# A new order table that moves forty plain transfers from SyncE's queue to ScalarE's, in a fused attention and gated-MLP kernel

## The chip, the core and the metric

The kernel runs on one core of a Trainium2 chip. The metric is the device time of one launch in microseconds (us). Five engines of the core take part: TensorE (PE, matrix products), VectorE (DVE), ScalarE (ACT), GpSimd (POOL) and SyncE (SP). SyncE computes nothing here: it only issues DMA transfers, one after the other, in program order. ScalarE issues transfers too, in its own program order and among its own arithmetic. Each engine takes its instructions strictly in the order in which the program lists them, so an instruction that waits holds back everything behind it on its engine.

## What is computed

```python
# q, k, v: (8, 12, 448, 64); w_in (768, 1024); conv_w (3, 1024); w_out (1024, 768)
q_n = q / sqrt(mean(q*q, -1) + 1e-6) * g_q          # the same for k with g_k
scores = q_n @ k_n.T / sqrt(64)
attn = exp(scores - max);  attn = attn / (sum(attn) + 1e-9)
x = (attn @ v).transpose(0, 2, 1, 3).reshape(8, 448, 768)
h = maximum(x @ w_in, 0)
conv_out = conv_w[0]*h[s-1] + conv_w[1]*h[s] + conv_w[2]*h[s+1]    # over the tokens s
out = (h * sigmoid(conv_out)) @ w_out               # (8, 448, 768), float32
```

## The kernel before

**Tiling.** The 96 heads are taken two at a time: 48 head pairs n = 0..47, six to a batch b. Pairs 0 to 9 work in float32 with their transposes on TensorE. From pair 10 on, everything that TensorE multiplies is split into two float16 parts (a rounded part and the remainder), and the transposes are done by DMA. A pair's probabilities are made in seven slots j of 128 rows. When a batch's six pairs are done, its tokens go through the MLP: a product with w_in (`in_part`, L1054), relu and the three-tap convolution (`in_relu`, L1062/L1064, and L1074), a gate through tanh (L1080), the product with w_out (`out_part`, L1123), the evacuation of the result (`out_evac`, L279/L281) and the store (`out_store`, L1137). Attention of later pairs and the MLP of earlier batches are interleaved, so that TensorE has matrix products from both.

**The path of one slot of probabilities** (pairs 10 on):

- `scores` (L836) multiplies q and k into a PSUM bank; `soft_max` (L842, DVE) takes the row maximum; `soft_exp` (L850, ACT) writes the exponentials into a tile `e` (ring of 4).
- `p_hi` (L855, recorded under the helper line L275, nearly always ACT) rounds `e` to float16 into the first half of a buffer `ph`; `p_lo` (L860, recorded under L287 as two instructions, POOL or DVE) puts the remainder into the second half.
- `p_turn` (L870, always SP) issues the DMA that transposes the `ph` buffer into the tile `PT`; after the last slot `pv` (L970) multiplies `PT` with v.
- `ph` has **four** buffers, used in turn by all slots. So `p_hi` of a slot can't start before the `p_turn` four slots earlier has landed.

`q_turn` (L700) is the same kind of transposing DMA for q, one for each pair from 10 on, also always on SP. There are 266 `p_turn` and 38 `q_turn`.

**Plain transfers.** All other transfers may be issued by SP or by ACT, as the table says for each of them (`issuer`): the loads of k and v (`load_k`, `v_load`, both L548), of q (`load_q`, L557 or L559), the softmax sums' way through memory to spread them over the partitions (`sum_store` L912, `sum_load` L926 from pair 10 on and L930 before), and the results (`out_store`). Before, 119 of them are issued by ACT.

**Completion semaphores.** Every transfer, of whichever engine, gets one of eight completion semaphores (DMAHW0 to DMAHW7), in turn, in program order. Before a transfer is issued, its engine has to know that the transfer eight places earlier, which used the same semaphore, has landed. Where an earlier wait of that engine doesn't already say so, the issue itself waits for it.

**What sets the order.** Nothing is scheduled while the kernel is built. The table `ORDER` (L20 on) has four characters for each of the 5038 steps: two name the step, one the engine, one the PSUM banks. It is decoded at L1248 to L1261, and L1268 to L1280 emit the steps in just that order. Each engine executes its steps as they come in the table. The code that matters for the steps spoken of later:

```python
phbuf = [const.tile([P, 2 * S], F16, name=f"ph{i}") for i in range(BUFS["ph"])]   # ph=4
...
def issuer(*step):
    return nc.scalar if on[step] == "ACT" else nc.sync
...
a, b, e, z = (DIGITS.index(x) for x in ORDER[4 * i : 4 * i + 4])
fn, args = plan[len(DIGITS) * a + b]
step, e = (fn.__name__, *args), ("PE", "DVE", "ACT", "POOL", "SP")[e]
order.append((step, fn))
on[step] = e
```

## Time and profile before

| | us |
|---|---|
| median of 3 runs | 843.84 |
| the three runs | 842.46, 843.84, 849.87 |
| the profiled execution, its own time | 841.89 |
| its span, first to last instruction | 840.0 |
| PE busy in the span | 770.5 (92%) |
| DVE busy | 706.2 (84%) |
| ACT busy | 677.3 (81%) |
| POOL busy | 467.2 (56%) |

How to read it: the three runs are timed without a profile; the profiled execution is a fourth one, and every row of the trace is of it. "Busy" counts arithmetic only. Issuing transfers isn't counted as busy, so SP has no busy time here; how long it is occupied is seen from the rows of its queue (SPq), where the duration of a transfer is the time that the *issue* takes on the engine, not the time to landing. In the same way ACTq is a transfer that ACT issues. In timelines and lists of waits, "[2.42 <-X]" says that the engine stood idle for 2.42 us before the instruction and that X ended the wait. The page divides the 840 us into 40 slices; in it, PE has something to do nearly everywhere, and no engine is full everywhere.

### The profile page before, as it was taken

What the parts mean: (1) busy time and instruction counts of PE and PEld (TensorE: products, weight loads), DVE (VectorE), ACT (ScalarE), POOL (GpSimd) and SP (SyncE); (2) the same over time, 40 slices, a digit from 0 to 9 for tenths busy, and PEclk for the clock granted to TensorE, in tenths of its full rate; (3) what the DMA queues carried; (4) which work ended last, traced back from release to release, by engine and by line L of the source; (5) the groups of instructions that cost most, each with busy time, mean ns of one, the idle gap of its engine ahead of it and who ended that gap; (6) DMA issues with size and microseconds to landing.
All of it is one profiled execution on the core that took longest, in us unless ns stands there. A gap on an engine that the chain in (4) does not pass through costs nothing.

```text
span 840.0 us, 16991 instructions
## 1 busy us (share of the span) xinstructions
PE 770.5 (92%) x5278; PEld 410.1 (49%) x5278; DVE 706.2 (84%) x1589; ACT 677.3 (81%) x1590; POOL 467.2 (56%) x758
## 2 busy tenths in 40 slices
...
GB/s 226 231 169 121 192 157 86 83 160 194 185 160 173 175 193 176 166 156 175 198 168 165 172 207 175 173 158 171 170 173 143 164 169 171 121 120 143 19 1 76
DMA packets 355246, 130.88 MB, mean 156 GB/s; under 512 B 297532, under 2 KB 351572, under 8 KB 355156
## 3 DMA queue, kind: packets, MB, share of 16 engines
...
## 4 chain that ended last, share of the span: by engine, by line
DMA 23%; ACT 21%; PE 18%; DVE 17%; POOL 9%; issue 8%; SPq 2%; ACTq 2%; POOLq 0%; DVEq 0%
DMA PT<-ph 17%; ACT e L850 7%; PE bank L1123 6%; POOL ph L287 5%; PE bank L1054 5%; ACT ph L275 4%; PE bank L970 3%; PE bank L836 3%; PE bank L878 2%; DMA qkf<-in_k_dram 2%; ACT sq L578 2%; DVE st L590 1%; DVE ph L287 1%; ACT bank L1062 1%; DVE vacc L744 1%
## 5 line engine op out<-in xcount | busy, mean ns | idle before, releaser
L287 POOL TENSOR_TENSOR ph<-e,ph 128x384 f16<-128x384 f32 x360 | 214.7, 623 | 90.1 <-ACT ph L275 37.0
L1054 PE MATMUL bank<-x,wi 128*128 128x448 f16 x1152 | 231.3, 356 | 3.1 <-ACT e L850 3.1
L1123 PE MATMUL bank<-wo,gring 128*128 128x384 f16 (+1 forms) x1056 | 197.2, 328 | 5.0 <-ACT e L850 2.1
L275 ACT CAST ph<-e 128x448 f16<-128x448 f32 x250 | 137.7, 565 | 47.2 <-DMA PT<-ph 42.7
L1054 PEld LDWEIGHTS <-wi 128*128 128x128 f16 x1152 | 111.4, 99 | 113.0 <-issue 19.0
L836 PE MATMUL bank<-kT,qT 64*128 64x448 f16 (+3 forms) x1072 | 140.3, 396 | 19.9 <-ACT e L850 11.2
L1123 PEld LDWEIGHTS <-gring 128*128 128x128 f16 (+1 forms) x1056 | 101.5, 99 | 75.2 <-issue 21.6
L287 POOL TENSOR_TENSOR sq<-qkf,st 112x512 f32<-112x512 f32 (+1 forms) x68 | 70.7, 1047 | 49.9 <-issue 14.4
L970 PE MATMUL bank<-PT,vp 128*64 128x448 f16 x836 | 87.0, 354 | 7.0 <-ACT e L850 4.7
L287 DVE TENSOR_TENSOR ph<-e,ph 128x384 f16<-128x384 f32 (+1 forms) x172 | 60.9, 396 | 19.7 <-ACT ph L275 17.6
L590 DVE TENSOR_REDUCE st<-sq 128x16 f32<-128x1024 f32 (+2 forms) x50 | 58.2, 1168 | 17.9 <-ACT sq L578 17.6
L970 PEld LDWEIGHTS <-vp 128*64 128x64 f16 x836 | 53.8, 109 | 38.8 <-issue 19.7
L836 PEld LDWEIGHTS <-qT 64*128 64x128 f16 (+1 forms) x912 | 35.0, 97 | 77.0 <-issue 57.1
L578 ACT ACTIVATE sq<-qkf 128x1024 f32<-128x1024 f32 (+2 forms) x47 | 48.1, 1024 | 18.6 <-DMA qkf<-in_k_dram 10.8
L658 PE MATMUL bank<-ident,sq 128*128 128x128 f32 (+1 forms) x232 | 35.3, 278 | 23.5 <-DVE sq L287 15.7
L287 POOL TENSOR_TENSOR qkf<-sq,qkf 112x512 f16<-112x512 f32 x34 | 39.4, 1160 | 16.0 <-ACT qkf L275 11.3
L1123 PE MATMUL bank<-wo,wi 128*128 128x384 f16 (+1 forms) x192 | 46.9, 326 | 0.0
L878 PE MATMUL bank<-ident,e 128*112 128x128 f32 x280 | 40.7, 284 | 6.0 <-ACT e L850 3.9
L658 PEld LDWEIGHTS bank<-ident,sq 128*128 128x128 f32 (+1 forms) x232 | 26.5, 143 | 35.8 <-issue 17.4
L878 PEld LDWEIGHTS bank<-ident,e 128*112 128x112 f32 x280 | 31.2, 137 | 23.1 <-ACT e L850 9.4
L287 POOL TENSOR_TENSOR x<-x,x 128x448 f16<-128x448 f32 x31 | 32.2, 1038 | 15.2 <-DVE rsum L900 3.2
L275 ACT COPY PT<-bank 112x512 f32<-112x512 f32 x66 | 36.9, 592 | 2.6 <-PE bank L878 2.6
...
## 6 DMA issues: line engine op xcount, KB each, us to landing
...
PT<-ph SPq DMA_TRANSPOSE x266
...
```

The lines of the kernel that those rows point to most:

```text
L275: (nc.scalar.copy if e == "ACT" else elementwise(e).tensor_copy)(dst, src)
L287: elementwise(e).tensor_tensor(dst, a, b, op=op)
L578: nc.scalar.activation(sq, x, AF.Square)
L590: nc.vector.tensor_reduce(st, sq, axis=AX.X, op=ALU.add)
L658: nc.tensor.transpose(ps[:, t * w : (t + 1) * w], x[:, t], ident[:w, :w])
L744: nc.vector.tensor_reduce(keyed(n, old("vacc", b))[:, i : i + 1], keyed(n, old("v", n)).rearrange("p h t d -> p (h t d)"), axis=AX.X, op=A ...
L836: nc.tensor.matmul(ps[u][o, :S], lhs, rhs, start=(i == 0), stop=(whole(m) or i == 2),)
L850: nc.scalar.activation(fixed("e", (n, j), ebuf)[:, :S], held["s", (n, j)][:, :S], AF.Exp, bias=old("sst", (n, j)), accum_out=old("rsum", n ...
L878: nc.tensor.transpose(ps[:w, kt * P : (kt + 1) * P], e[:, kt * w : (kt + 1) * w], ident)
L970: nc.tensor.matmul(ps[HALF[h], :S], lhs, pt[:, k, h * S : (h + 1) * S], start=(i == 0 and j == 0), stop=(i == pvs(n)[-1] and j == NB - 1),)
L1054: nc.tensor.matmul(ps[:, :S], wi[:, wl, c, fc * P : (fc + 1) * P], old("x", b * NP + c)[:, xl], start=(i == 0), stop=(i == 3 * NP - 1),)
L1123: nc.tensor.matmul(ps[p0 : p0 + m, :NO2], g, wo[:, wl, fc, half * NO2 : (half + 1) * NO2], start=(i == 0), stop=(i == 3 * NFC - 1),)
```

## The change

Only the table `ORDER` is new; no function and no buffer changes. Both tables hold the same 5038 steps. Three things differ:

- **Issuers.** 90 plain transfers (as steps of the table) move from SP to ACT and 50 from ACT to SP: 159 instead of 119 are issued by ACT. Between the first and the last `p_turn`, SP has 198 plain DMA instructions in its order before and 149 after (`p_turn` and `q_turn` not counted), ACT 104 and 153.
- **Places.** Steps stand in another order. Most of the moved transfers stand later behind the release of the buffer that they fill, or behind the step whose result they store.
- **Engines of arithmetic.** 245 of the other steps change engine, in both directions and nearly in balance: 73 from DVE to POOL and 70 back, 39 from ACT to DVE and 32 back, 19 from POOL to ACT and 12 back.

```diff
--- before.py
+++ after.py
 ORDER = (
-    "$6&!$8$!!!#!$9#!$7&!$C$!$:#!$;#!$<%!$=%!$D#!$E#!$>#!!:&!!>#!$?#!$T&!$F#!$G%!$U#!%$&!%&$!%%&!$@%!"
...
+    "$6&!$8$!!!#!$7&!$C$!!:&!$9#!$:#!$;#!$<%!$=%!$D#!$E#!!>#!$F#!$>#!!?#!$G#!$?#!$H%!$T&!$U#!%$&!%&$!"
...
 )
```

What that does to the engines' queues is shown at three places.

**First place: SP, at head pair 21.** SP's instructions from the end of pair 20's `p_turn`s into those of pair 21. `PT_20`/`PT_21` is the transposed tile of the pair, `ph0` to `ph3` the four buffers of the ring, `qkf` the float32 tiles of q and k, `v4`/`v5` tiles of v, `rd` the memory through which the softmax sums go, `row` the tile that they come back to. Before:

```order
L870 DMA_TRANSPOSE PT_20_3990<-ph0_77 128x7x128
L548 DMA qkf1_86<-in_k_dram 64x2x256
L870 DMA_TRANSPOSE PT_21_4182<-ph1_78 128x7x128
L557 DMA qkf1_86<-in_q_dram 112x2x128 x2
L548 DMA v4_92<-in_v_dram 64x2x256
L548 DMA v4_92<-in_v_dram 64x2x192
L1137 DMA out_0_dram<-c_('o'_1_3_1_4066 128x384
L700 DMA_TRANSPOSE qT_23_4220<-qkf2_87 128x8x112
L870 DMA_TRANSPOSE PT_21_4182<-ph2_79 128x7x128
L870 DMA_TRANSPOSE PT_21_4182<-ph3_80 128x7x128
L548 DMA qkf2_87<-in_k_dram 64x2x256
L912 DMA rd_20_4309<-rT_20_4283 4x32x32
```

and after:

```order
L870 DMA_TRANSPOSE PT_20_3980<-ph0_77 128x7x128
L548 DMA qkf1_86<-in_k_dram 64x2x192
L557 DMA qkf1_86<-in_q_dram 112x2x128 x2
L870 DMA_TRANSPOSE PT_21_4212<-ph1_78 128x7x128
L870 DMA_TRANSPOSE PT_21_4212<-ph2_79 128x7x128
L700 DMA_TRANSPOSE qT_23_4252<-qkf2_87 128x8x112
L870 DMA_TRANSPOSE PT_21_4212<-ph3_80 128x7x128
L870 DMA_TRANSPOSE PT_21_4212<-ph0_77 128x7x128
L870 DMA_TRANSPOSE PT_21_4212<-ph1_78 128x7x128
L548 DMA qkf2_87<-in_k_dram 64x2x256
L548 DMA v5_93<-in_v_dram 64x2x256
L912 DMA rd_21_4366<-rT_21_4314 4x32x32
```

Before, two loads of q, two of v, a store and a `q_turn` stand between the first and the second `p_turn` of pair 21. After, nothing stands between these two, and only the `q_turn` between the second and the third. The loads of v and the store that stood here have moved, some of them to ACT.

**Second place: ACT, at head pairs 34 to 36.** ACT's instructions with what each waits for; DMAHW is one of the eight completion semaphores. Before:

```order
L850 ACTIVATE e0_81,rsum0_96<-bank6_72,sst_(36_0_7368 128x448 [waits DVE_49]
L548 DMA qkf1_86<-in_k_dram 64x2x256 [waits DMAHW6_49]
L275 CAST ph1_78<-e3_84 128x448 [waits DMAHW0_49,Activation_49]
L850 ACTIVATE e1_82,rsum0_96<-bank3_69,sst_(36_1_7394 128x448 [waits DVE_49,Pool_49]
L926 DMA row0_98<-rd_34_7268 4x1x448 [waits DMAHW2_49]
L275 CAST ph2_79<-e0_81 128x448 [waits DMAHW1_49,Activation_49]
L275 CAST ph3_80<-e1_82 128x448 [waits Activation_49]
```

and after:

```order
L850 ACTIVATE e3_84,rsum1_97<-bank6_72,sst_(35_6_7315 128x448 [waits DVE_49,Activation_49,Pool_49]
L926 DMA row0_98<-rd_34_7264 4x1x448 [waits DMAHW6_49,DMAHW5_49]
L275 COPY vp_34_7135<-vp_34_7135 64x2x64
L275 COPY carry_102<-gring_101 128x2x64 x2
L850 ACTIVATE e0_81,rsum0_96<-bank2_68,sst_(36_0_7322 128x448 [waits DVE_49,Activation_49,Pool_49]
L548 DMA qkf1_86<-in_k_dram 64x2x256
L275 CAST ph0_77<-e2_83 128x448 [waits DMAHW7_49,Activation_49]
L275 CAST ph1_78<-e3_84 128x448 [waits DMAHW0_49,Activation_49]
L1137 DMA out_0_dram<-c_('o'_4_1_0_7221 128x384
```

The `sum_load` of pair 34 (L926) has moved up by two exponentials and now waits for two semaphores. The load of k, which waited for a semaphore before, waits for nothing after.

**Third place: DVE, up to the first product that TensorE needs.** L397, L401 and L405 convert one part of a weight, L590 to L632 make the root mean squares of q and k (tile `st`), L1173 and L1174 the gains, and L287 with the tile `sq` scales q and k; TensorE's first transposes need that. The rows go up to the first scaling. Before (one L397 stands further ahead):

```order
L401 SCALAR_TENSOR_TENSOR wi32_99<-wo32_100,wi32_99 128x512
L617 SCALAR_TENSOR_TENSOR st_0_111<-st_0_111 112x8 x2
L405 SCALAR_TENSOR_TENSOR wi32_99<-wo32_100,wi32_99 128x512
L590 TENSOR_REDUCE st_1_141<-sq_1_142 112x8
L1173 TENSOR_TENSOR G_75<-gqk_74 128x1
L1174 TENSOR_SCALAR G_75<-G_75 128x1
L617 SCALAR_TENSOR_TENSOR st_0_111<-st_0_111 112x8 x2
L625 TENSOR_SCALAR st_1_141<-st_1_141 112x8
L287 TENSOR_TENSOR sq_0_112<-qkf0_85,st_0_111 112x2x4x64
```

and after (a first L397, L401 and L405 stand further ahead):

```order
L397 TENSOR_SCALAR wi32_99<-wo32_100 128x512
L617 SCALAR_TENSOR_TENSOR st_0_111<-st_0_111 112x8
L623 TENSOR_SCALAR st_1_143<-st_1_143 112x8
L617 SCALAR_TENSOR_TENSOR st_0_111<-st_0_111 112x8
L401 SCALAR_TENSOR_TENSOR wi32_99<-wo32_100,wi32_99 128x512
L617 SCALAR_TENSOR_TENSOR st_0_111<-st_0_111 112x8
L625 TENSOR_SCALAR st_1_143<-st_1_143 112x8
L590 TENSOR_REDUCE st_1_143<-sq_1_144 112x8
L1173 TENSOR_TENSOR G_75<-gqk_74 128x1
L1174 TENSOR_SCALAR G_75<-G_75 128x1
L287 TENSOR_TENSOR sq_0_112<-qkf0_85,st_0_111 112x2x4x64 x2
```

The L397 and the L401 shown of after are a second conversion's, and stand ahead of the first scaling only now; the second scaling follows the first at once ("x2"), where before other steps stood between them.

## Rows read from the trace of the kernel before

**Rows 1.** The page, part 1: busy us (share) and instructions of each engine.
```profile
PE 770.5 (92%) x5278; PEld 410.1 (49%) x5278; DVE 706.2 (84%) x1589; ACT 677.3 (81%) x1590; POOL 467.2 (56%) x758
```

**Rows 2.** The page, part 4: the chain that ended last, by line.
```profile
DMA PT<-ph 17%; ACT e L850 7%; PE bank L1123 6%; POOL ph L287 5%; PE bank L1054 5%; ACT ph L275 4%; PE bank L970 3%; PE bank L836 3%; PE bank L878 2%; DMA qkf<-in_k_dram 2%; ACT sq L578 2%; DVE st L590 1%; DVE ph L287 1%; ACT bank L1062 1%; DVE vacc L744 1%
```

**Rows 3.** Windows: stretch, us, busy (x) of PE, PEld, DVE, ACT, POOL; PEclk, DMA share, GB/s.
```profile
115.00:767.00 652.00, 610.69 (x4301) 324.00 (x4299) 575.89 (x1298) 563.99 (x1327) 407.62 (x649) 0.99 0.87 164
200.00:560.00 360.00, 335.96 (x2417) 178.86 (x2415) 320.33 (x721) 317.71 (x744) 232.97 (x373) 0.99 0.95 176
```

**Rows 4.** Waits: engine, line, waited for; us in total, times, longest.
```profile
ACT ph L275 <- DMA PT<-ph: 42.7, 42, 3.2
POOL ph L287 <- ACT ph L275: 37.0, 29, 4.8
```

**Rows 5.** SP's issues, first row whole run, others 200:560: count, ns min/median/max, first start.
```profile
L870 SPq DMA_TRANSPOSE PT<-ph x266: 1220/1245/2987, 161.7 to 767.2; - x133
...
L870 SPq DMA_TRANSPOSE PT<-ph x156: 1220/1247/2987, 199.9 to 560.0; - x156
...
L700 SPq DMA_TRANSPOSE qT<-qkf x23: 1221/1253/2312, 203.9 to 553.0; - x23
...
L548 SPq DMA_DIRECT2D v<-in_v_dram x31: 595/607/741, 246.0 to 559.2; - x31
L548 SPq DMA_DIRECT2D qkf<-in_k_dram x29: 595/632/794, 208.4 to 548.9; - x29
```

**Rows 6.** Timeline at 339 to 346 us, SP and one POOL row: start, duration.
```profile
338.99 1.23 SPq L870 DMA_TRANSPOSE PT<-ph  x1
...
340.32 1.04 SPq L557 DMA_DIRECT2D qkf<-in_q_dram  x2
340.54 1.18 POOL L287 TENSOR_TENSOR ph<-e,ph 128x384 f16<-128x384 f32 x2
...
341.41 1.26 SPq L548 DMA_DIRECT2D v<-in_v_dram  x2
...
342.72 0.58 SPq L1137 DMA_DIRECT2D out_dram<-c_('o'_1_3_1_4066  x1
...
343.42 1.31 SPq L700 DMA_TRANSPOSE qT<-qkf  x1
...
344.85 3.06 SPq L870 DMA_TRANSPOSE PT<-ph  x2
```

**Rows 7.** Timeline at 578 to 584 us, ACT's queue, ACT and PE.
```profile
578.19 0.56 ACTq L926 DMA_DIRECT2D row<-rd  x1
578.84 0.56 ACT L275 CAST ph<-e 128x448 f16<-128x448 f32 x1 [3.22 <-DMA PT<-ph]
...
583.56 0.66 PE L658 MATMUL bank<-ident,sq 128*128 128x128 f32 x4 [3.11 <-ACT ph L275]
```

**Rows 8.** Timeline of ACT: the first and the last of ten waits behind an issue.
```profile
290.59 1.03 ACT L275 CAST ph<-e 128x448 f16<-128x448 f32 x2 [2.20 <-DMA PT<-ph]
...
664.65 1.06 ACT L578 ACTIVATE sq<-qkf 128x1024 f32<-128x1024 f32 x1 [1.95 <-DVE vacc L744]
```

**Rows 9.** Timeline of ACT at 326 us: an issue that nothing is held back by.
```profile
326.18 0.60 ACTq L548 DMA_DIRECT2D qkf<-in_k_dram  x1
326.33 0.58 ACT L1080 ACTIVATE c_(2_0_3914<-c_(2_0_3914 128x448 f32<-128x448 f32 x1
```

**Rows 10.** Windows (columns as in Rows 3): the low-clock stretches between 300 and 600 us.
```profile
318.40:321.80 3.40, 3.40 (x11) 1.37 (x9) 2.56 (x8) 2.38 (x8) 1.64 (x5) 0.51 0.70 126
...
441.30:444.70 3.40, 3.40 (x11) 1.37 (x11) 3.39 (x8) 3.40 (x9) 2.66 (x5) 0.50 0.49 133
...
584.70:588.10 3.40, 3.40 (x20) 1.36 (x13) 3.30 (x11) 2.91 (x8) 2.06 (x3) 0.50 1.07 180
```

**Rows 11.** Timeline of DVE at the start: the first two conversion steps.
```profile
8.66 0.43 DVE L397 TENSOR_SCALAR wi<-wo 128x512 int32<-128x512 int32 x1 [2.50 <-DMA wo<-in_moe_w_in_dram]
...
10.06 0.68 DVE L401 SCALAR_TENSOR_TENSOR wi<-wo,wi 128x512 int32<-128x512 int32 x1
```

More of the change, by code (lines that the diff above doesn't have):

```diff
@@ new lines @@
+    "$I#!$J%!%(#!$@%!!@#!$K#!$A#!!;&!!C#!$B#!%)#!%%&!!A$!!4&!$L#!!D#!!<&!%2$!!=&!$M#!%q&!%*#!%+%!%,%!"
+    "%3#!!5#!%4%!$Q#!$N#!%5#!$R!#%-#!!E#!$S$!%6#!%r&!$O!$$P$!!H#!%C&!%7#!!F$!!M#!!I#!!N#!%8#!!J#!%.%!"
+    "%/%!!B&!%D#!%9%!!K$!$V!B$Y#!$Z$!!O#!!G&!%0#!!L&!$^#!!Q&!%:%!!R#!%;#!$W!V$c#!%<#!!S#!&S&!&T&!%1#!"
+    "!W#!%=%!%s$!$g#!$[!*%t#!$X!n$k#!%@%!!X#!!]#!$o#!$_$!!c#!&(&!$]$!$d$!$a!$$h$!$e!%$i!&!T#!!d#!&^&!"
+    "(B&!(y&!!Y#!!V&!$b$!%>!*$f$!$j$!%A!(%?$!%B$!%E![!^#!$s#!$l$!!_#!$p$!&U$!(/&!&V#!(0&!$m!%$n$!$q!&"
@@ new lines @@
+    "$r$!%I#!$t$!$w%!%u%!%F!i!e#!%v#!%w%!%x%!%y%!![&!%z%!%{%!%|%!!P$!%M#!$x#!)a&!&)#!!Z$!$u!+!3%!$v$!"
+    "$y#!!a$!%Q#!%G!/$}!&&_#!%U#!!l#!!f$!%}#!!h#!%~%!%J$!%N$!&$%!%K!)%O!+&W%!%R$!%S!$!U$!(C#!%Y#!%V$!"
+    "%L$!#,&!(z#!!b&!%H!i%P$!%T$!%^#!$z&!({#!%Z$!%c#!!i#!!m#!&!!#&#$!(o&!(p&!!j#!${&!&%!)&&$!&Z%!%_$!"
+    "%d$!%g%!(|!+&X!$&*!?&-#!(1$!(}#!&1#!$|&!(2#!$~#!%W!)&.$!&+!i&5#!&[!+*:&!(q%!(r#!&9#!&Y$!%X$!%!%!"
+    "%#%!%[!%%a!$&]$!(3%!!p#!%]$!(4#!%h#!%e!)(5%!(6%!&,!p&=#!!g&!%i#!!t#!&2$!%b$!&/!&&3!#&6$!!q#!%f$!"
```

408 lines of the change are left out of this document (199 added, 209 removed).

## The prediction

> **What bounds the kernel now.** I read the page's busy line first. TensorE is busy for 770.5 of 840 us [rows 1], so even a perfect order can't give more than about 70 us. Then the windows. In the long middle, 115 to 767 us, TensorE is busy for 610.69 of 652 us [rows 3]: 41.3 us of idle time in many short pieces. No stretch is badly filled, and the other engines have room too (ScalarE is busy for 317.71 of 360 us at 200 to 560 us) [rows 3]. So what can be won lies in those 41 us and in the slow-clock stretches that follow some of them.
>
> What makes the pieces? The chain that ended last says which work the end is held by: 17% of it is the transposing DMA of the probabilities, 5% is `p_lo` on GpSimd and 4% is `p_hi` on ScalarE [rows 2]. These three are one loop: `p_hi` fills one of four `ph` buffers, `p_lo` completes it, `p_turn` must land before `p_hi` gets the buffer again. The list of waits says that the loop is closed at ScalarE: `p_hi` waited 42 times for a `p_turn`, 42.7 us in all, and `p_lo` on GpSimd waited 37.0 us for `p_hi` [rows 4]. While ScalarE waits there, its next exponentials wait too, and TensorE's scores behind those.
>
> Why is a `p_turn` late? SyncE's rows at 200 to 560 us: 156 `p_turn` of 1.247 us, 23 `q_turn` of 1.253, 31 loads of v of 0.607, 29 of k of 0.632 [rows 5]. That is 194.5 + 28.8 + 18.8 + 18.3 = 260 of 360 us, 72%, before loads of q, sums and stores are counted. A queue so full makes what is in it late. One case: `p_lo` of pair 21's second slot ended at 340.54 + 1.18 = 341.72 us, but SyncE was in two loads of q, then issued two of v, a store and a `q_turn`; the `p_turn` went out at 344.85, 3.1 us late [rows 6].
>
> A second cost is ScalarE's own issues. An issue whose semaphore is still held by a transfer eight places earlier stops ScalarE. At 578.19 us a `sum_load` was issued so late that ScalarE had stood for 3.22 us, and TensorE then stood for 3.11 [rows 7]. I find ten such stops between 289 and 665 us, of 1.95 to 3.22 us, with some 16 us beyond the issues' own time [rows 7, 8].
>
> **The change, part by part.**
>
> *SyncE's queue.* Between the first and the last `p_turn` SyncE loses 49 plain issues. At 0.60 us (loads of v and k, [rows 5]) that is 29.4 us of queue time. How much reaches the end? Three readings. (a) The loop holds 17 + 5 + 4 = 26% of the chain [rows 2]; 29.4 x 0.26 = 7.6 us. (b) The loop's 26% of 840 us is 218 us, all of it inside the 605 us from the first to the last `p_turn`, 161.7 to 767.2 [rows 5]; 218/605 = 0.36, which gives 10.6. (c) The relief is spread over 266 `p_turn`s, 0.11 us each; the chain spends 17% of 840 = 143 us in such DMAs, at about 3 us apiece some 48 of them, and 48 x 0.11 = 5.3. I take 8: reading (c) is too low where the order empties the queue just ahead of a `p_turn`, as at pair 21 in the first place of the change, and (b) too high where the landing itself is awaited. Bounds: 3 (only some of the 42 waits of [rows 4] were queue) and 17 (42.7 us of waits of which 0.4 goes).
>
> *ScalarE's forty more issues.* The trace shows an issue of 0.60 us at 326.18 and ScalarE's next arithmetic at 326.33, inside it [rows 9]. So an issue that needn't wait hides beside arithmetic, and I cost it at nothing; the cover is ScalarE's arithmetic on either side. Without that cover it is 40 x 0.60 = 24 us of ScalarE time, which has 360 - 317.71 = 42 us of slack in the 360 us of [rows 3]; that is the upper bound, and it is in the rivals.
>
> *ScalarE's stops.* In the new order 22 of the close cases are left of 27 (ScalarE issues whose semaphore belongs to a SyncE transfer with under about 3.4 us of ScalarE work between). 16 us x 5/27 = 3 us fewer. TensorE lost 3.11 of 3.22 in the case of [rows 7] and nothing at others, so two thirds: -2. Bounds 0 and -6. At the second place of the change both directions are seen: the load of k loses its wait, the `sum_load` gains one.
>
> [...]
>
> *The other moves.* The 245 steps of arithmetic that change engine nearly cancel: no engine gains more than about 2 us, and none is the bound. At the start, two more conversion steps stand ahead of the first scaling on VectorE, 0.43 + 0.68 = 1.1 us [rows 11]. VectorE had stood for 2.50 us before the first conversion [rows 11], so part of it is waiting for data anyway, and the second scaling comes sooner; I take +0.6 of 0 to 1.1. The tail, after the last `p_turn`, is TensorE's, and its work is the same: 0, with 1 either way.
>
> *Sum.* -8 - 2 - 2.5 + 0.6 = -11.9 us. Against the profiled execution's own 841.9 us that is 830.0. The median of the runs shown lies 2.0 above that execution, so I forecast 832 for the runs. As a cross-check, TensorE's idle time at 115 to 767 would fall from 41.3 to about 31.
>
> **The rivals.**
>
> [...]
>
> *No gain, since the transfers themselves are the limit.* The 16 DMA engines are busy to 0.95 at 200 to 560 us [rows 3], and the change takes no byte away; moving the issue from one queue to the other would then only shift the waiting. The loads that are issued sooner by ScalarE would fall beside the transposes and slow them. The 0.95 speaks for it; against it speaks [rows 6], where 3.1 us passed before the transfer was even issued. Price: the 8 us of the first term don't come, and the rest is between -4 and +1: 840 to 845. [...]
>
> *Slower: ScalarE stops at its own issues.* ScalarE's issues whose semaphore was last used by a SyncE transfer rise from 55 to 68. If the thirteen added ones stop it for 2.4 us each, about the middle of the 1.95 to 3.22 us of [rows 7, 8], that is 31 us, two thirds on the path: +21, less the 8 won: 843.8 + 13 = 857. From five such stops on (5 x 2.4 x 2/3 = 8 us) the gain of the queue is gone; from about ten the kernel is measurably slower. Against it: by the order fewer of these issues are close (22 for 27).
>
> *The change does nothing to the queue* can't be: 49 issues are gone from it by count.
>
> **How the numbers follow.** About 1% (8.4 us) is what a measurement of this kernel can tell from no change, so faster means under 835.4 and slower over 852.2. Forecast (826 to 838): 0.47. Bigger gain (815 to 826): 0.12. No gain (838 to 846): 0.25. Slower (847 to 862): 0.16. Faster takes the bigger gain and most of the forecast: 0.12 + 0.40 = 0.52. Slower by over 1% takes most of its rival: 0.13. The rest, 0.35, is within 1%. The range for 8 in 10 goes from 820 (a third of the bigger gain, 0.04, left out) to 847 (the slower rival, 0.16, left out). The forecast's own range is 826 to 838, which holds the bounds of the smaller terms.
>
> **What would show it.** Right, if after the change: the wait of `p_hi` for its `p_turn` falls from 42.7 us [rows 4] to about 33; the loop's share of the chain falls from 26% to 22% or less; TensorE's idle time at 115 to 767 is near 31; low-clock stretches are one or two instead of three; ScalarE's stops behind issues are eight or fewer; SyncE's share at 200 to 560 is several points lower; the first scores start within 1 us of before. Wrong: if SyncE's rows are sparser but `p_hi` still waits 40 us and more for landings, the transfers were the limit; if ScalarE shows more than fifteen stops of 2 us or more ahead of its own issues, the slower rival came; if the stalls go from `p_hi` to the scores or to the loads of k (now issued later), the order only moved them.

## The result and the profile after

The changed kernel takes 813.75 us (median of 4 runs: 811.13, 811.95, 815.55, 817.84) against 843.15 us before (median of its three runs and the profiled one): a ratio of 0.964, 95% interval 0.957 to 0.971. That is 30 us less, where I had forecast 12 and a range that ended at 820. The profiled execution is the slowest of the four, 817.84 us with a span of 814.9; every row of after is of it.

The page of after, parts 1 and 4, busy time and the chain by line, answers to [rows 1, 2]:

```profile
PE 763.4 (94%) x5278; PEld 403.8 (50%) x5278; DVE 702.9 (86%) x1591; ACT 674.5 (83%) x1590; POOL 467.0 (57%) x752
...
PE bank L1123 14%; PE bank L1054 11%; DMA PT<-ph 9%; ACT e L850 7%; PE bank L970 4%; ACT ph L275 4%; PE bank L836 4%; DMA qkf<-in_q_dram 2%; POOL ph L287 2%; ACT sq L578 2%; ACTq L548 1%; DMA gring<-in_moe_w_out_dram 1%; DVE st L590 1%; DVE ph L287 1%; DMA wo<-in_moe_w_in_dram 1%
```

The loop of `p_hi`, `p_lo` and `p_turn` falls from 26% of the chain to 9 + 2 + 4 = 15%, and TensorE's two MLP products (L1123, L1054) rise from 11% to 25%. The windows of after (columns as in [rows 3]):

```profile
0.00:115.00 115.00, 91.64 (x532) 50.23 (x532) 103.16 (x246) 96.28 (x234) 49.16 (x94) 1.00 0.67 185
115.00:767.00 652.00, 627.32 (x4450) 330.01 (x4449) 585.13 (x1322) 567.55 (x1338) 410.79 (x650) 0.99 0.89 166
200.00:560.00 360.00, 339.32 (x2454) 177.63 (x2455) 325.03 (x731) 320.26 (x749) 234.38 (x374) 1.00 0.97 179
767.00:814.90 47.90, 44.40 (x300) 23.57 (x297) 14.64 (x25) 10.64 (x20) 7.09 (x8) 1.00 0.10 34
```

and the first and last of the same windows of before:

```profile
0.00:115.00 115.00, 90.79 (x526) 48.73 (x527) 102.79 (x241) 94.42 (x229) 49.68 (x96) 0.97 0.67 184
...
767.00:840.00 73.00, 69.03 (x455) 37.36 (x452) 27.51 (x53) 18.92 (x35) 9.93 (x14) 1.00 0.14 43
```

From these the whole 25.1 us between the two spans can be laid out. TensorE's idle time was 24.2 + 41.3 + 4.0 = 69.5 us and is 23.4 + 24.7 + 3.5 = 51.6: 17.9 less, nearly all of it in the middle. Its busy time for the same matmuls is 770.5 - 763.4 = 7.1 less. A part of that is the clock. The stretches of after that the trace's record of the clock has at the lower level, while TensorE works:

```profile
433.20:436.60 3.40, 3.40 (x10) 1.37 (x9) 3.23 (x7) 3.40 (x10) 2.90 (x7) 0.50 0.72 136
682.30:685.70 3.40, 3.40 (x12) 1.14 (x9) 3.16 (x12) 3.33 (x9) 1.26 (x6) 0.51 0.82 152
```

against the three of [rows 10] and one more of before, twice as long, that I hadn't counted:

```profile
72.70:79.50 6.80, 6.53 (x25) 3.17 (x26) 5.84 (x15) 5.29 (x15) 3.41 (x8) 0.50 0.40 116
```

That is 17.0 us at the lower level before and 6.8 after. Within these stretches each of L1054's matmuls starts 373 ns after the one ahead of it (median, in both traces), outside of them 189 ns: at the full clock the work in the missing 10.2 us takes half, 5.1 us. But the record of the clock only begins at 21.49 us before and at 30.45 after, and the windows count what is ahead of it as full speed. TensorE's rows of after say that it wasn't, for the same four matmuls on either side of that point:

```profile
25.17 1.87 PE L836 MATMUL bank<-kT,qT 64*128 64x448 f32 x4
...
33.59 1.02 PE L836 MATMUL bank<-kT,qT 64*128 64x448 f32 x4
```

Up to those two points TensorE has 5.96 us of work before and 11.40 after, so the longer slow start takes some 2.7 us back (an estimate: half of the difference). The clock as a whole gave about 2.4 of the 7.1 us; the rest isn't placed.

The waits of after (engine, line, waited for; us, times, longest), against [rows 4], and TensorE's first work, of after and then of before:

```profile
POOL ph L287 <- ACT ph L275: 39.3, 31, 4.3
...
ACT ph L275 <- DMA PT<-ph: 24.4, 25, 2.7
```

```profile
15.63 1.73 PE L658 MATMUL bank<-ident,sq 112*128 112x112 f32 x8 [15.63 <-DVE sq L287]
18.09 2.61 PE L836 MATMUL bank<-kT,qT 64*128 64x448 f32 x6 [0.72 <-ACT kT L279]
```

```profile
13.33 0.98 PE L658 MATMUL bank<-ident,sq 112*128 112x112 f32 x4 [13.33 <-DVE sq L287]
...
17.49 4.49 PE L836 MATMUL bank<-kT,qT 64*128 64x448 f32 x12 [0.62 <-ACT qT L275]
```

`p_hi` waits 18 us less for its `p_turn`. Last, SyncE's queue at the place of [rows 6], from pair 21's first transpose on:

```profile
330.36 3.10 SPq L870 DMA_TRANSPOSE PT<-ph  x2
333.56 1.24 SPq L700 DMA_TRANSPOSE qT<-qkf  x1
335.19 4.96 SPq L870 DMA_TRANSPOSE PT<-ph  x3
```

The pair's first two `p_turn` go out one behind the other, both within 3.10 us; before, the second started 5.9 us after the first (338.99 and 344.85).

So the direction and the signs were right, and the size was not. Two theories were to be told apart. **Theory Q**: SyncE's queue time is what costs, and a microsecond less of it is worth something in any order. **Theory P**: order, issuers and engines of arithmetic only work together, because each engine runs its list strictly in order; taking one wait away in a given order only lets the engine run up to the next one.

### The profile page after: what moved, and what is told of

The parts are those of the page before. It is cut to its first block, busy times and chain, and to the rows that moved or that the text cites. A ratio compares the mean times of both kernels' runs of the same rounds, so it can differ in the third digit from the quotient of the medians.

```text
span 814.9 us, 16968 instructions
## 1 busy us (share of the span) xinstructions
PE 763.4 (94%) x5278; PEld 403.8 (50%) x5278; DVE 702.9 (86%) x1591; ACT 674.5 (83%) x1590; POOL 467.0 (57%) x752
## 4 chain that ended last, share of the span: by engine, by line
PE 34%; ACT 20%; DMA 16%; DVE 15%; issue 7%; POOL 4%; ACTq 2%; SPq 1%; DVEq 0%; POOLq 0%
PE bank L1123 14%; PE bank L1054 11%; DMA PT<-ph 9%; ACT e L850 7%; PE bank L970 4%; ACT ph L275 4%; PE bank L836 4%; DMA qkf<-in_q_dram 2%; POOL ph L287 2%; ACT sq L578 2%; ACTq L548 1%; DMA gring<-in_moe_w_out_dram 1%; DVE st L590 1%; DVE ph L287 1%; DMA wo<-in_moe_w_in_dram 1%
## 5 line engine op out<-in xcount | busy, mean ns | idle before, releaser
L287 POOL TENSOR_TENSOR ph<-e,ph 128x384 f16<-128x384 f32 x364 | 217.6, 623 | 84.7 <-ACT ph L275 39.3
L1054 PE MATMUL bank<-x,wi 128*128 128x448 f16 x1152 | 233.1, 356 | 5.6 <-ACT e L850 5.5
L1123 PE MATMUL bank<-wo,gring 128*128 128x384 f16 (+1 forms) x1056 | 196.3, 327 | 0.6 <-ACT e L850 0.6
L1054 PEld LDWEIGHTS <-wi 128*128 128x128 f16 x1152 | 110.7, 98 | 116.0 <-issue 23.8
L275 ACT CAST ph<-e 128x448 f16<-128x448 f32 x251 | 138.8, 564 | 28.9 <-DMA PT<-ph 24.4
L836 PE MATMUL bank<-kT,qT 64*128 64x448 f16 (+3 forms) x1072 | 136.6, 391 | 12.5 <-ACT e L850 9.0
L1123 PEld LDWEIGHTS <-gring 128*128 128x128 f16 (+1 forms) x1056 | 100.4, 99 | 70.1 <-issue 16.6
L287 POOL TENSOR_TENSOR sq<-qkf,st 112x512 f32<-112x512 f32 (+1 forms) x65 | 67.2, 1043 | 42.2 <-DVE st L617 9.0
L287 DVE TENSOR_TENSOR ph<-e,ph 128x384 f16<-128x384 f32 (+1 forms) x168 | 59.3, 395 | 11.1 <-ACT ph L275 10.2
L970 PEld LDWEIGHTS <-vp 128*64 128x64 f16 x836 | 49.5, 110 | 37.2 <-issue 14.2
L590 DVE TENSOR_REDUCE st<-sq 128x16 f32<-128x1024 f32 (+2 forms) x50 | 58.3, 1168 | 10.6 <-ACT sq L578 10.3
L836 PEld LDWEIGHTS <-qT 64*128 64x128 f16 (+1 forms) x912 | 33.7, 97 | 67.3 <-issue 49.2
L287 POOL TENSOR_TENSOR qkf<-sq,qkf 112x512 f16<-112x512 f32 x34 | 39.4, 1160 | 23.7 <-DVE ph L287 8.1
L658 PE MATMUL bank<-ident,sq 128*128 128x128 f32 (+1 forms) x232 | 35.0, 279 | 17.6 <-DVE sq L287 15.6
L1123 PE MATMUL bank<-wo,wi 128*128 128x384 f16 (+1 forms) x192 | 46.9, 326 | 0.0
L287 POOL TENSOR_TENSOR x<-x,x 128x448 f16<-128x448 f32 x32 | 33.2, 1038 | 15.0 <-DVE ph L287 6.1
```

The lines of the kernel that those rows point to most:

```text
L275: (nc.scalar.copy if e == "ACT" else elementwise(e).tensor_copy)(dst, src)
L287: elementwise(e).tensor_tensor(dst, a, b, op=op)
L590: nc.vector.tensor_reduce(st, sq, axis=AX.X, op=ALU.add)
L658: nc.tensor.transpose(ps[:, t * w : (t + 1) * w], x[:, t], ident[:w, :w])
L836: nc.tensor.matmul(ps[u][o, :S], lhs, rhs, start=(i == 0), stop=(whole(m) or i == 2),)
L970: nc.tensor.matmul(ps[HALF[h], :S], lhs, pt[:, k, h * S : (h + 1) * S], start=(i == 0 and j == 0), stop=(i == pvs(n)[-1] and j == NB - 1),)
```

## The experiments

All are timed against the kernel before in the same session. "New" and "old" say which table a part is from. "us" is 843.8 times (ratio - 1). Where the order is new and the arithmetic is new, the 245 steps that change engine have gone along with the order; the places alone, with old issuers and old engines, were not run.

| kernel | order | issuers | arithmetic | ph | median us | ratio, 95% interval | us |
|---|---|---|---|---|---|---|---|
| changed kernel | new | new | new | 4 | 813.75 | 0.964, 0.957 to 0.971 | -30.4 |
| e1 | new | old | new | 4 | 834.43 | 0.989, 0.985 to 0.994 | -8.9 |
| e2 | old | new | old | 4 | 840.06 | 0.994, 0.992 to 0.996 | -5.0 |
| e5 | old | old, 90 more on ScalarE | old | 4 | 844.56 | 1.000, 0.998 to 1.003 | 0 |
| e9 | old | old, 9 to SyncE | old | 4 | 839.57 | 0.996, 0.993 to 0.998 | -3.7 |
| e16 | new | new, 50 back to ScalarE | new | 4 | 827.74 | 0.980, 0.974 to 0.985 | -17.3 |
| e17 | new | new, 90 back to SyncE | new | 4 | 837.90 | 0.993, 0.990 to 0.996 | -6.2 |
| e7 | new | k, v old | new | 4 | 821.47 | 0.973, 0.968 to 0.978 | -22.8 |
| e8 | new | all but k, v old | new | 4 | 820.81 | 0.971, 0.967 to 0.976 | -24.3 |
| e6 | new | new | old | 4 | 854.00 | 1.011, 1.005 to 1.016 | +8.9 |
| e11 | old | old | new | 4 | 858.59 | 1.020, 1.015 to 1.024 | +16.5 |
| e3 | old | old | old | 5 | 837.48 | 0.993, 0.990 to 0.996 | -5.7 |
| e14 | old | new | old | 5 | 829.11 | 0.982, 0.979 to 0.985 | -15.2 |
| e13 | new | old | new | 5 | 831.97 | 0.987, 0.980 to 0.993 | -11.3 |
| e4 | new | new | new | 5 | 804.80 | 0.953, 0.949 to 0.957 | -39.7 |
| e15 | old | old, 15 to SyncE | old | 5 | 837.36 | 0.992, 0.988 to 0.995 | -7.1 |
| e12 | new | new, 5 to SyncE | new | 5 | 803.54 | 0.952, 0.948 to 0.955 | -40.7 |
| x1 | new to step 3230, then old | | | 4 | 825.51 | 0.982, 0.977 to 0.986 | -15.5 |
| x2 | old to step 3227, then new | | | 4 | 829.73 | 0.987, 0.981 to 0.993 | -11.2 |

Two numbers worked out from the traces go with them. The first is how late a `p_turn` is: from the end of the `p_lo` that completes its buffer to the start of its issue, a mean over all 266. The second is ScalarE's waits at 115 to 740 us (of all its steps, not of `p_hi` alone), added up from the rows of its list of waits by what ended them.

| kernel | p_turn late, us | ScalarE waits | for p_turn's DMA | other DMA | VectorE | rest |
|---|---|---|---|---|---|---|
| before | 1.55 | 74.4 | 46.6 | 8.1 | 13.6 | 6.1 |
| e2, issuers only | 1.16 | 73.4 | 33.8 | 6.5 | 16.3 | 16.8 |
| e3, five ph | 2.14 | 76.3 | 25.6 | 15.8 | 19.0 | 15.9 |
| e5, 90 to ScalarE | 0.87 | 79.2 | 23.7 | 14.2 | 24.0 | 17.3 |
| e14, issuers, five ph | 1.36 | 64.9 | 13.0 | 9.9 | 23.9 | 18.1 |
| e1, order only | 1.67 | 68.5 | 34.8 | 14.8 | 10.9 | 8.0 |
| e13, the same, five ph | 1.93 | 67.6 | 17.6 | 21.3 | 14.9 | 13.8 |
| e6, old arithmetic | 0.87 | 75.4 | 26.1 | 3.6 | 32.7 | 13.0 |
| e16, 50 back to ScalarE | 0.76 | 65.0 | 24.8 | 7.3 | 16.4 | 16.5 |
| e17, 90 back to SyncE | 2.16 | 75.3 | 50.1 | 9.6 | 5.2 | 10.4 |
| after | 1.00 | 57.2 | 24.4 | 9.8 | 9.6 | 13.4 |
| e4, the same, five ph | 1.31 | 56.8 | 8.4 | 13.0 | 10.3 | 25.1 |

### Order or issuers (e1, e2)

Each of the 382 plain transfers gets its issuer from a string of its own, with the other table's choice; in e2 it is laid over the old table. (These two kernels are seven lines longer, so L836 is L843 in their rows.)

```diff
+ISSUERS = (
+    "000000000000000000000000000000000000000000000000000000000000010001110000100000110000001000101000"
...
         step, e = (fn.__name__, *args), ("PE", "DVE", "ACT", "POOL", "SP")[e]
+        if fn.__name__ in PLAIN:
+            e = ("SP", "ACT")[int(ISSUERS[plain.index(len(DIGITS) * a + b)])]
```

> The new order with the old issuers: each of the 382 plain transfers is issued by the engine that issued it before (119 by ScalarE), everything else is the new table. Theory Q (the gain is SyncE's queue time, so many issues of 0.60 us less): most of the gain goes, 830 to 840 us, and the waits of p_hi for p_turn come back to about 40 us. Theory O (the gain is where the steps stand, so that what a queue holds is asked for later): 813 to 820 us, and the waits of p_hi stay near 24 us.

> The old order with the new issuers: 159 plain transfers on ScalarE, each where the old table has it. Theory Q: most of the gain comes, 818 to 830 us. Theory O: nothing or worse, 838 to 860 us, because transfers that ScalarE now issues stand in the old order right behind what they wait for, and ScalarE stops at them.

The order (with its engines of arithmetic) gives 8.9 us without the issuers, the issuers alone give 5.0, both 30.4: some 16 us come only when both are new. With five `ph` buffers it is the same: 5.6 and 9.5 us one by one, counted from e3 to e13 and e14, and 34.0 together (e4). e1 came out where theory Q had it and e2 where theory O had it, so neither theory holds as it stands. In e2, SyncE's relief is there, and `p_hi` waits 10 us less for its transposes than the 42.7 of [rows 4]:

```profile
ACT ph L282 <- DMA PT<-ph: 32.2, 33, 2.9
...
DVE rB L942 <- DMA row<-rd: 14.2, 7, 3.9
```

but VectorE now waits 14.2 us for the softmax sums, against 3.4 before; 12.8 of them end with a `sum_load` that ScalarE issued. The sum of ScalarE's waits stays at 73.4.

### More relief in the old order (e5), and the places where ScalarE stops (e9)

The fourth part of a step's entry in the table is its engine: "&" is SyncE, "$" ScalarE, "#" VectorE, "%" GpSimd. One of 90 entries of e5 and one of nine of e9:

```diff
-    ")l!*)p!()s$!#Z&!)m$!#+%!)q$!)E&!#Y$!-(&!+L$!#[#!,%&!,&$!*<!B)~#!)H!+(m%!(n%!+M#!*l%!)t!*)w$!)x!("
+    ")l!*)p!()s$!#Z&!)m$!#+%!)q$!)E&!#Y$!-($!+L$!#[#!,%&!,&$!*<!B)~#!)H!+(m%!(n%!+M#!*l%!)t!*)w$!)x!("
...
-    "3!$!1h$!2S#!5|&!2N$!2T&!2}!I4F#!4G#!5}$!4H%!3&#!3($!4I#!7v$!7##!3,#!31#!3#$!7$!)N{!!N|!!N}!!N~!!"
+    "3!$!1h$!2S#!5|&!2N$!2T&!2}!I4F#!4G#!5}$!4H%!3&#!3($!4I#!7v&!7##!3,#!31#!3#$!7$!)N{!!N|!!N}!!N~!!"
```

> The old order; the 90 transfers that the change moves from SyncE to ScalarE are moved, the 50 that go the other way stay on ScalarE: 209 on ScalarE. SyncE gets 90 issues less instead of 40. Theory Q (SyncE's queue time is what costs, whatever the order): twice the relief of the run with the new issuers alone and more, 815 to 832 us. Theory P (order and issuers only work together: in the old order ScalarE stops at transfers that stand too close behind what they wait for): 835 to 850 us, with more than twelve ScalarE stops of over 0.6 us ahead of an issue.

> The kernel before with nine of its 119 ScalarE transfers given to SyncE where they stand: those at whose issue ScalarE stood for 0.8 us or more (14.7 us in all) between 115 and 767 us. Theory S (the long stalls of the old order start where ScalarE stops at its own issue, and everything that waits for ScalarE goes with it): 828 to 836 us, with TensorE's idle time at 547 to 590 us falling from 5.8 us to under 3. Theory Q (SyncE's queue is what costs; nine more issues make it worse): 843 to 850. If both are true in part: 836 to 843.

e5 is the clearest blow to theory Q, and to the way in which I had priced the change. SyncE has 90 issues less, and its issues fill 76% of 200 to 560 us instead of 89%; its `p_turn`s are late by 0.87 us instead of 1.55, `p_hi` waits 22.8 us instead of 42.7, and the time is 844.56: nothing. That is the net of the relief and of what the 90 issues cost on ScalarE; the two were not parted. Rows of e5, from the list of waits and from the timeline of ScalarE, show what took the place:

```profile
ACT ph L275 <- DMA PT<-ph: 22.8, 25, 2.7
```

```profile
545.04 1.26 ACTq L548 DMA_DIRECT2D v<-in_v_dram  x2
546.35 0.58 ACT L1080 ACTIVATE c_(4_3_6815<-c_(4_3_6815 128x448 f32<-128x448 f32 x1 [3.61 <-issue]
```

ScalarE stops at two loads of v that it now issues where the old order has them, and stands for 3.61 us. Twelve such stops of over 0.6 us are in the trace at 115 to 740 us (18.1 us, counted between the end of ScalarE's work and its issue), nine in that of before (14.7 us).

e9 takes those nine away: three are left (4.0 us), and the time falls by 3.7 us. So taking them away gave about a third of their length, with the nine issues added to SyncE's queue paid out of it (1.4 to 6.1 us by the interval), and not the two thirds I had taken from [rows 7].

### The other direction in the new order (e16, e17), and by kind (e7, e8)

One entry each of e16 (50), e17 (90), e7 (70) and e8 (70):

```diff
-    "!8&!*C$!*G$!#f&!#@$!+U#!!+%!-{&!*,!)*P#!*M$!*T#!*Q$!*x%!*y!+*z$!*u%!,>#!*J!**K$!)K%!,&&!*X#!*v!$"
+    "!8&!*C$!*G$!#f&!#@$!+U#!!+%!-{&!*,!)*P#!*M$!*T#!*Q$!*x%!*y!+*z$!*u%!,>#!*J!**K$!)K%!,&$!*X#!*v!$"
...
-    "*o%!)}$!)I#!*?!L*$$!*F!$#c#!)J$!*p#!*H#!#T$!*q%!*r%!*&#!#a&!#g#!*I$!#d#!*s#!#h#!*t#!-&&!-($!*L#!"
+    "*o%!)}$!)I#!*?!L*$$!*F!$#c#!)J$!*p#!*H#!#T$!*q%!*r%!*&#!#a&!#g#!*I$!#d#!*s#!#h#!*t#!-&&!-(&!*L#!"
...
-    ",J%!/C&!/E&!L/$!L:$!L;$!+z#!L0#!.[#!K~$!,E%!+F!),L#!L<#!-j%!+D&!+E&!,Q#!/Y&!L!%!L1$!-k#!/Z&!LH!!"
+    ",J%!/C&!/E$!L/$!L:$!L;$!+z#!L0#!.[#!K~$!,E%!+F!),L#!L<#!-j%!+D&!+E&!,Q#!/Y&!L!%!L1$!-k#!/Z&!LH!!"
```

(The second pair stands in e7 and in e17 alike.)

> The changed kernel with the 50 transfers that the change moved from ScalarE to SyncE back on ScalarE: 209 on ScalarE, SyncE's queue 50 issues or some 30 us emptier. Theory Q: faster than the changed kernel, 795 to 810 us. Theory P (those 50 stand in the new order where ScalarE can't issue them without a stop): 816 us or more, with more than ten ScalarE stops of over 0.6 us.

> The changed kernel with the 90 transfers that the change moved to ScalarE back on SyncE: 69 on ScalarE, SyncE's queue 90 issues or some 54 us fuller. Theory Q, by the 20.7 us for 40 in the run with all old issuers: 840 to 865 us. If it costs no more than those (the count isn't what matters): 830 to 838.

> The changed kernel with the old issuers for the loads of k and v only (70 steps; 127 transfers on ScalarE instead of 159, so 32 of the 40 go back to SyncE). Theory Q, by the run with all old issuers (20.7 us for 40, 0.52 us each): 813.75 + 16.6 = 830, at least 825. If the other kinds (sums, stores, q) matter more, because other steps wait for them: under 822.

> The changed kernel with the old issuers for everything but the loads of k and v (sums, stores, loads of q; 70 steps, 151 on ScalarE, so 8 of 40 go back). Theory Q: 813.75 + 8 x 0.52 = 818, at most 821. If the place matters and not the count (an exchange of issuers in a table that was laid out for others spoils it): 822 or more, with little change in SyncE's occupation.

Both directions are slower. With 50 issues less in SyncE's queue (e16) the `p_turn`s are the least late of all, 0.76 us, and the kernel loses 13 of its 30 us: twelve ScalarE stops (15.7 us) against six after the change (9.6), and VectorE is waited for 16.4 us instead of 9.6. With 90 more (e17) it loses 24. Here the queue shows, since `p_hi` waits twice as long, but not at theory Q's price: the 40 of e1 had already cost 21.5. The row of e16, and under it that of e17:

```profile
ACT ph L275 <- DMA PT<-ph: 22.3, 24, 2.3
```

```profile
ACT ph L275 <- DMA PT<-ph: 53.3, 52, 3.0
```

The count of issues isn't what decides: 32 of the 40 given back (e7) cost 7.6 us by the ratios, the other 8 (e8) cost 6.1, and all 40 at once (e1) 21.5. Nor do `p_hi`'s waits set the time: they are 35.6 us in e7 and 32.6 in e1, and e7 is 14 us faster. So in the new order a fuller queue of SyncE goes with a slower kernel; whether an emptier one would help isn't shown, because in e16 ScalarE's stops came with it.

### The arithmetic that I had priced at nothing (e6, e11)

One of the 245 entries of e6; e11 is the mirror, on the old table.

```diff
-    "%/%!!B&!%D#!%9%!!K$!$V!B$Y#!$Z$!!O#!!G&!%0#!!L&!$^#!!Q&!%:%!!R#!%;#!$W!V$c#!%<#!!S#!&S&!&T&!%1#!"
+    "%/%!!B&!%D#!%9%!!K$!$V!B$Y#!$Z$!!O#!!G&!%0#!!L&!$^#!!Q&!%:%!!R#!%;#!$W!V$c#!%<%!!S#!&S&!&T&!%1#!"
```

> The changed kernel with the arithmetic engines of before: the 245 steps of arithmetic that change engine go back, order and issuers stay new. If the 245 are worth nothing, as I priced them: 811 to 820 us. If they carry part of the gain (each placed where its new engine has room): 822 to 840 us.

> The old order and issuers with the new arithmetic engines for the 245 steps. If the new engines are simply better placed (a balance of VectorE and GpSimd): 815 to 838 us, the mirror of the 40 us that the old engines cost in the new order. If an order only fits the engines that it was laid out for (theory P): 855 us or more here too.

This is the largest effect of all, and it was missing in my sum. The new order with the old arithmetic engines is 39 us slower than the new kernel, and slower than before, outside both of the ranges that I had given. Yet e6's `p_turn`s are less late than after the change (0.87), and `p_hi` waits as long (24.2 us). The old order with the new engines is 16.5 us slower than before, so the new engines are not better ones; they belong to their order. In e6 ScalarE waits 32.7 us for VectorE. The page of e6, then the rows of VectorE's larger `p_lo` instruction, of e6 and of before (count; busy, mean ns of one; idle before):

```profile
PE 774.9 (91%) x5278; PEld 405.4 (48%) x5278; DVE 723.0 (85%) x1589; ACT 681.4 (80%) x1590; POOL 482.9 (57%) x758
```

```profile
L287 DVE TENSOR_TENSOR ph<-e,ph 128x384 f16<-128x384 f32 x86 | 53.4, 620 | 16.5 <-ACT ph L275 12.8 <-issue 3.1 <-POOL st L630 0.4
```

```profile
L287 DVE TENSOR_TENSOR ph<-e,ph 128x384 f16<-128x384 f32 x86 | 48.5, 564 | 19.7 <-ACT ph L275 17.6 <-DMA PT<-ph 1.8
```

VectorE and GpSimd have the same work in e6 as in the kernel before, and it takes VectorE 16.8 us and GpSimd 15.7 us longer (706.2 and 467.2 in [rows 1]). The traces show where: the larger `p_lo` takes 551 ns in the mean in both kernels where GpSimd did nothing during it (57 times in e6, 67 before, never over 560), and 757 ns in e6 against 610 before where GpSimd was at work beside it (29 and 19 times). Over all instructions of VectorE and GpSimd that occur with the other engine idle too, those that ran beside the other engine's work took 24.6 and 21.1 us more than the median of the undisturbed ones in e6, 21.7 and 16.4 in e11, and 6.9 and 7.4 before, 5.8 and 7.5 after. So in e6 and e11 the two engines' instructions lose 46 and 38 us beside each other, and with each table's own engines 14 and 13.

One thing else differs in these two, and I had overlooked it in the kernel: by the lists at L1234 to L1241 and the lines up to L1280 some steps of GpSimd are made to wait for the last step of VectorE on a second list. Before and after have 152 such pairs, e6 has 190 and e11 has 191. So the 39 us are the price of the engines together with these waits; how much of it is the slower instructions and how much the added waits wasn't parted.

### Five ph buffers (e3, e4, e13, e14), and fewer stops with them (e15, e12)

```diff
-        qkf=3, sq=2, st=2, qT=2, kT=2, v=8, sst=6, e=4, PT=2, x=12, c=3,
-        rB=2, x32=1, vacc=2, vsc=4, cwb=3, rd=2, rsum=2, rT=1, row=1, ph=4, vp=2,
+        qkf=3, sq=2, st=2, qT=2, kT=2, v=8, sst=6, e=4, PT=2, x=11, c=3,
+        rB=2, x32=1, vacc=2, vsc=4, cwb=3, rd=2, rsum=2, rT=1, row=1, ph=5, vp=2,
```

e13 and e14 are this with the issuers of e1 and e2; e15 and e12 are e3 and e4 with fifteen and five entries turned to "&", as in e9.

> The kernel before with five ph buffers instead of four; room for it comes from x, which has 11 buffers instead of 12. Theory L (the loop p_hi, p_lo, p_turn over four buffers is what the end is held by): the 42.7 us of waits of p_hi for p_turn fall under 15 and the time falls by 15 to 30 us, to 813 to 828. If the loop is only where a delay shows that something else sets: the waits move to another line and the time stays within 838 to 848.

> The changed kernel with five ph buffers (and 11 of x). Theory L: the 24.4 us of waits that are left fall under 10 and the time falls by another 5 to 15 us, to 798 to 809. If the new order has already opened the loop: within 3 us of 813.75.

> The new order with the old issuers (as in the run with the order only, 834 us) and five ph buffers, 11 of x. If in the new order the late p_turns are all that the old issuers cost: it comes back to 812 to 820 us. If the old issuers also make other transfers late (q_turn, loads, sums): 824 to 832.

> The old order with the new issuers (840 us) and five ph buffers, 11 of x. Theory P (in the old order one wait only takes the place of another): 832 us or more. If the two reliefs add up to what the change gives: 815 to 826 us.

> The kernel before with five ph buffers, 11 of x, and the fifteen transfers at which ScalarE stood for over 0.6 us in the run with five buffers given to SyncE. If those stops swallowed the gain of the fifth buffer: 820 to 829 us. If the old order has yet another wait behind them: 831 to 840 us.

> The changed kernel with five ph buffers, 11 of x, and the five transfers at which ScalarE stood in the run of that kernel given to SyncE. Each stop was 0.66 to 3.3 us, 8.1 in all, of which a third to two thirds should reach the end: 799 to 803 us against 804.8.

e3 opens the loop in the old order: `p_hi`'s waits fall from 42.7 to 14.7 us, as theory L wanted, and the time by 5.7 us only. From its list of waits, and from that of e4 below it:

```profile
ACT ph L275 <- DMA PT<-ph: 14.7, 13, 2.6
...
ACT sq L578 <- DMA qkf<-in_q_dram: 7.6, 6, 2.2
```

```profile
ACT ph L275 <- DMA PT<-ph: 6.6, 8, 1.6
...
ACT sq L578 <- DMA qkf<-in_q_dram: 4.0, 4, 2.2
```

In e3 the `p_turn`s are even later than before (2.14 us), ScalarE stops fourteen times (22.4 us), and its waits add up to 76.3. Giving the fifteen transfers to SyncE (e15) leaves eight stops (12.2 us) and gains no more than the intervals allow. In e4 the same buffer takes 9 us off the changed kernel. With the new issuers the fifth buffer is worth 10 us in the old order (e2 to e14) and 9 in the new; with the old ones 6 and 2. So a deeper ring pays with the new issuers, where the `p_turn`s are 1.3 to 1.4 us late and not 1.9 to 2.1. e14 goes against theory P, which had 832 us or more for it: its two reliefs give 15.2 us in the old order, and ScalarE's waits do fall, to 64.9. e13 says what the old issuers cost in the new order apart from the ring: with 17.6 us of waits for `p_turn`s, fewer than after the change, it is 28 us slower than e4, and ScalarE's waits for other DMAs stand at 21.3 us. From its list:

```profile
ACT sq L578 <- DMA qkf<-in_k_dram: 10.7, 6, 5.6
ACT ph L275 <- DMA PT<-ph: 10.1, 10, 2.6
...
ACT sq L578 <- DMA qT<-qkf: 5.4, 1, 5.4
```

e12, 803.54 us, and e4, 804.80, are the two fastest versions; their intervals don't part them.

### Where in the program (x1, x2)

```diff
-order = old
+order = new[:3230] + [s for s in old if s not in new[:3230]]      # x1
...
+order = old[:3227] + [s for s in new if s not in old[:3227]]      # x2
```

(This says what the table holds; it is written out as a table. At this place, 58% of TensorE's work, the two tables have done the same steps but for nine.)

> A splice: the new table's first 3230 steps (58% of TensorE's work, to about 525 us), then the old table for the rest; 28 PSUM banks of later steps are renamed so that none is overwritten while it is in use. By the comparison of the two traces the new kernel is about 10 us ahead there, the rest of its lead comes later. If the gain is made locally, at a few stalls: 833 to 838 us. If the old part needs nothing of what the new one prepares or spoils it: outside of 828 to 842.

> The other splice: the old table's first 3227 steps, then the new table for the rest; 8 banks renamed. If the gain is local: 843.8 less the 16 to 19 us that the new order gains after that point, 824 to 829 us, and the savings of the two splices add up to about the 29 us of the change. If it is global: they don't add up, by more than 6 us.

By the ratios the two parts give 15.5 and 11.2 us, 26.7 together, against 30.4 for the whole: they add up within their intervals, as e1 and e2 don't. Windows of before, after, x1 and x2, in this order:

```profile
115.00:525.00 410.00, 385.56 (x2729) 206.19 (x2727) 367.08 (x827) 365.29 (x860) 260.80 (x412) 0.99 0.88 167
525.00:740.00 215.00, 198.60 (x1391) 103.06 (x1389) 185.11 (x413) 180.45 (x424) 135.81 (x220) 0.99 0.87 161
```

```profile
115.00:525.00 410.00, 389.25 (x2759) 205.00 (x2758) 372.07 (x841) 369.68 (x868) 263.94 (x412) 1.00 0.92 171
525.00:740.00 215.00, 211.07 (x1522) 110.46 (x1522) 198.68 (x448) 193.10 (x461) 141.74 (x230) 0.99 0.91 168
```

```profile
115.00:525.00 410.00, 394.10 (x2797) 208.09 (x2796) 379.46 (x856) 376.13 (x886) 270.04 (x423) 1.00 0.92 173
525.00:740.00 215.00, 202.61 (x1443) 105.78 (x1442) 189.05 (x427) 181.78 (x429) 132.73 (x215) 1.00 0.86 158
```

```profile
115.00:525.00 410.00, 381.10 (x2659) 202.66 (x2658) 359.60 (x812) 358.50 (x841) 259.40 (x407) 0.98 0.89 166
525.00:740.00 215.00, 211.24 (x1529) 110.30 (x1528) 200.13 (x445) 197.07 (x467) 144.08 (x233) 0.99 0.91 169
```

Where the table is new, TensorE is idle for 16 to 21 us of 410 and 4 of 215; where it is old, for 24 to 29 and 12 to 16. No dependence of one half on the other is seen beyond those intervals. x1's first part is step for step that of after and does 5 us more work in the same window; so single executions differ by that much, and x1's expectation, made from one trace, was 8 us too high.

## Why the prediction was wrong

**The bound: right as far as it went.** ScalarE's waits for `p_turn`s went from 42.7 to 24.4 us (forecast about 33), the loop's share of the chain from 26% to 15% (22 or less), TensorE's idle time at 115 to 767 from 41.3 to 24.7 (31), ScalarE's stops from nine to six by the measure used above, and the share of 200 to 560 us that SyncE's issues fill from 89% to 84%. All the signs that I had named for "right" came, most of them larger than I had said.

**The step that failed** is "How much reaches the end?", together with "The other moves". I took the change for 29.4 us of SyncE's time and asked which part of it counts, with the order held fixed; the order and the arithmetic I priced at nothing. The runs show it the other way round. The issuers with the order fixed are worth 5.0 us (I said 8, within its bounds of 3 to 17). The order with the old issuers is worth 8.9, where I had 0. Both together are worth 16 us more than the two singly, and a sum of terms that are each priced in the old order has no place for that. And the arithmetic engines, 0 in my sum because no engine gained busy time, cost 39 us when they are put back; VectorE is then busy for 20 us longer than after the change, which a count of moved steps doesn't show.

**Why the parts don't add.** In the old order ScalarE's waits stay at 73 to 79 us when one wait is relieved: by fewer issues (e2), a deeper ring (e3) or 90 issues less (e5). What is taken from the wait for the transposes comes back as a wait for VectorE, for other transfers or at its own issues. With two reliefs at once (e14) they fall to 64.9. In the new order the waits for VectorE don't rise when the transposes come sooner (10.9 in e1, 9.6 after), and the sum falls to 57. That a single relief is mostly swallowed in the old order is shown by the runs. Why is not: I take it that ScalarE's next steps stand in its list where the old pace lets them be ready, but which of the steps' new places makes room wasn't found, since the places were only tried in two halves. What the share of the chain measures is how often the end hung on the loop, not what would be next in its place.

**ScalarE's stops, -2.** Six are left of nine, 9.6 of 14.7 us; by e9's rate of a third that is 1.7 us. The size was right by luck, out of two errors: more stops went than forecast, and each is worth less than [rows 7] led me to think.

**The clock, -2.5.** It gave about 2.4, and that is luck too. No run shows the clock frequencies that I worked this term out from; what the traces show in their place is a granted clock of 0.50 to 0.51 [rows 10] and L1054's 373 ns against 189, by which the three stretches of [rows 10] cost about 5 us. I counted three stretches between 300 and 600 us and left out the longest recorded one, 6.80 us at 72.7; the recorded ones gave 5.1, and the longer slow start, which I hadn't thought of, took 2.7 back.

**The start, +0.6.** It cost 2.3: TensorE began at 15.63 instead of 13.33 us. I had added two conversions (1.1 us) and overlooked what else stands ahead of the first scaling now: one more reduction of the next pair (L590, the fourth where three stand ahead before) with its small steps. The listings at my third place begin too late to show the three that both orders have. VectorE's timeline of before and of after:

```profile
12.50 0.68 DVE L287 TENSOR_TENSOR sq<-qkf,st 112x512 f32<-112x512 f32 x1
```

```profile
13.95 0.68 DVE L590 TENSOR_REDUCE st<-sq 112x8 f32<-112x512 f32 x1
...
14.80 1.28 DVE L287 TENSOR_TENSOR sq<-qkf,st 112x512 f32<-112x512 f32 x2
```

The second scaling follows at once, and by the first scores (18.09 against 17.49 us) 0.6 of the 2.3 is left, the number that I had taken. But that isn't what the start costs. With the slow start, after has done at 48.5 us what before had done at 45, by TensorE's work added up from the traces; it is ahead from about 80 us on, when the stretch at 72.7 has held before back.

**The rivals.** "Bigger gain" (815 to 826) came nearest by the number, and I gave it 0.12: 40% of TensorE's idle time at 115 to 767 us went. That slack in SyncE's queue alone would free so much is not borne out: e2 and e5 have the slack and not the gain. "No gain, since the transfers are the limit" falls: the DMA share at 200 to 560 us rose to 0.97, and to 1.00 in e4 at 804.80 us; a share of 0.95 was no ceiling. In e5 SyncE's time for 90 issues was saved, 76% of 200 to 560 us instead of 89%, and nothing came of it, because other waits took its place; after the change the same kind of saving, to 84%, is part of 30 us. "Slower: ScalarE stops at its own issues" did not come with the change, but ScalarE's stops are more in e16 and e5.

**What stays open.** Of the 16 us that need both, no single transfer or step is named. e13 shows that they aren't the ring of `ph` alone: with five buffers the old issuers still cost 28 us in the new order.
